# The first norm's second step and the scale of g called in the middle of the first group, and four more weight tiles ordered one behind the other, on one core

## The chip, the core and the metric

The kernel runs on one core of a Trainium2 chip. TensorE (PE in the profile) multiplies matrices, and loads their stationary side as PEld; VectorE (DVE), ScalarE (ACT) and GpSimd (POOL) work element by element; the queues of SyncE (SP), ScalarE and GpSimd issue the DMA transfers. The metric is the device time of one execution, in microseconds.

## The reference

Three layers follow one another, on 4 sequences of 576 tokens:

```python
attn = softmax(q @ k.T / 8 + cum[:, None] - cum[None, :], causal)   # 8 heads of 64; cum = cumsum(log f)
x  = heads joined to 512 columns of attn @ v
xn = (x - mean(x)) / sqrt(var(x) + 1e-6) * g_ln
x2 = x + relu(xn @ w_ch1) @ w_ch2                 # 512 x 2048 and 2048 x 512
u, v = split(relu(x2 @ w_in))                     # 512 x 1024
out = (u * (w_spatial @ layernorm(v) + b)) @ w_out
```

The weights of the MLPs arrive as 64-bit floats.

## The kernel before, in words

**Tiling.** The 2304 tokens are cut into nine blocks of 256 tokens (first, second and third part of a sequence, and a last block of leftovers). `BLOCKS` names their order. Attention of a block (`attention32` for the first two, `attention1` for the next two, `attention` for the rest) gives xT, 512 columns on partitions by 256 tokens. `GROUPS` makes eight groups of them, seven of one block and one of two; `mlp` runs the first MLP on a group. It has 16 steps j, one for each 128 of the 2048 hidden columns: the first layer into a bank ph (L858), relu into hh (L869, and hl at L873, what hh as a 16-bit number leaves over), the second layer into the banks acc (L843) two steps behind (`AHEAD`). Two banks hold ph, two hold acc. At a group's end the accumulators are scaled into t and added to x2 in memory (L890 or L892, and the DMA behind it).

**Precision.** The first group multiplies in fp32 with the weights as they are. All later groups multiply three times in fp16, with weights and inputs each as a high and a low part. xh and xl (L822) are the two parts of x, scaled by gs, one power of two times g.

**Weights.** The 16 weight tiles of 1 MB come as raw 64-bit words, three buffers deep. `load_w` converts tile j through `narrow`: ScalarE takes the upper word (L653) and the lower word (L654), VectorE clips (L655), fetches the sign (L656) and joins the two (L657). TensorE then sums the squares of a converted tile (L707, `squares`), and `scales` works out the two scales w1c and w2c from them when all tiles are there. `make16` halves a tile into its fp16 parts with them (ScalarE, and VectorE at L741).

**The first norm.** The first group doesn't wait for its norm: `norm`'s first step takes only the mean away from x times g, and keeps the mean in `kept`. The factor y, which is 1/sqrt(var + eps) for each token, is multiplied in at the end (L892). y comes out of the norm's second step: centre x (L776), square it (L782, ScalarE), two sums on GpSimd (L786, L787), a mean on TensorE, logarithm and exponential (L790, L791) and three corrections on VectorE (L792 to L794). The same lines serve the norm of every other block, where their c is xT with av in place of `kept`.

**The scale of g.** `gscale` loads g once more, 256 KB over all partitions, through GpSimd's queue (L249), takes the largest entry (L251), makes a power of two of it (L253, L261 to L263) and multiplies g by it (gs, L255). xh and xl need gs, and `scales` needs gsc.

**The order.** `run` gives every piece of work a number on a common axis, where the first group has 0 to 1, and calls the pieces sorted by it. A scheduler puts the instructions on each engine's queue in the order of the calls, its own estimate of when each can start, and the pairs that the code names with `after(later, earlier)`, which fixes an order and adds no work. The event that this case is about is

```python
events += [(at, -2, j) for j, at in enumerate(RAWAT)] + [(REST, -1, -1), (DEC, -1, -2)]
...
elif n < 0:
    drain(self.rest)
    self.gscale()
```

`self.rest` is the first norm's second step. The conversions of the tiles from 5 on stand at (j - 4.5)/17 on the axis, so 0.7 lies behind the one of the last tile, 15 (0.62); `scales` is at 0.76, the first halvings at 0.765. The names qk, s, sd, st, P, PT, vr, vp, vs, vq and vsc are attention's: scores s from qk (L530), a masked minimum (L535), P in two parts (L546), its transpose PT, and the product av<-PT,vp (L555), copied to xT (L556). vgram and vtr belong to a scale of v.

Of the kernel before, what the change touches and what calls it, by code (L numbers as in the profile page):

```python
# [57 lines left out]
PACE = (1, "x3", "split", "split", "split")  # L58
LOWAT = (1, "x3", "split")
SUMS = 14  # L60
REST = 0.7
SQ = (1, 3, 4, 5, 6, 8, 9, 10, 12, 13, 14, 16)
SOON = 5
WSC, MAKE, VN = 0.76, 0.765, 0.82
# [24 lines left out]
class Kernel:  # L89
# [586 lines left out]
    def load_w(self, j):  # L676

        nc = self.nc
        if j not in self.raw:
            self.load_raw(j)  # L680
        raw, w = self.raw.pop(j), self.wt[:, j + 2]
        low = self.st.tile([P, 2 * DM], U32, tag="low", name="low", bufs=2)
        joined = self.joined if 0 < j < 4 else None
        for hf in range(1 if j else 2):
            c = slice(0, 2 * DM) if j else slice(hf * DM, hf * DM + DM)
            first = self.narrow(raw[:, c], w[:, c], low[:, c], self.marks["split"] if hf else joined if j else self.marks["PT2"])
            if j == hf == 0:
                self.decays32(self.joined)
            for ins, pace in ((first, PACE), (self.low, LOWAT)):
                at = "x3" if hf else pace[j] if j < len(pace) else NP + j - len(pace) if ins is first else None  # L690
                if at is not None:
                    self.after(ins, self.marks[at] if isinstance(at, str) else self.done[at])
        self.marks[f"low{j}"] = self.low
        if j == 1:
            self.marks["w1"] = self.joined
        if j == 2:
            self.marks["third"] = self.joined
# [497 lines left out]
    def run(self):  # L1195
# [91 lines left out]
        events += [(WSC, -1, NF + 1)] + [(VN + 0.04 * i, -1, NF) for i in range(B + 2)]  # L1287
        events += [(at, -2, j) for j, at in enumerate(RAWAT)] + [(REST, -1, -1), (DEC, -1, -2)]
        events += [(BEGIN[-2] + M2A + (e + 0.5) / M2S, 2, last) for e in range(26)]
# [154 lines left out]
```

## Time and profile before

| | us |
|---|---|
| median of 3 runs | 788.42 (787.94 to 788.70) |
| the profiled execution | 784.56 |
| its span in the profile | 782.6 |
| TensorE busy | 754.1 |
| VectorE busy | 558.3 |
| ScalarE busy | 524.1 |

The first line is what is measured without a profile. The profiled execution is a single one; its span is from its first to its last instruction, and 2.0 us of its own time lie outside. The mean granted clock of TensorE over it was 0.991 of full speed. The first group runs to about 110 us, the second from there to 189 us.

### The profile page before, as it was taken

How to read it: one execution, taken by the hardware profiler on the slowest of the kernel's cores; microseconds unless marked ns; L12 is line 12 of the kernel's file. 1: busy time of each engine (PE TensorE's matmuls, PEld its weight loads, DVE VectorE, ACT ScalarE, POOL GpSimd, SP SyncE). 2: the span in 40 equal slices, each digit the busy share in tenths (PEclk: the TensorE clock that was granted, in tenths of full speed). 3: DMA queues.
4: the chain of work that ended last, by engine and by line, in shares of the span. 5: the costliest groups of instructions: out<-in, count | busy, mean ns of one | idle time of the engine just before them, and what ended most of it. 6: DMA issues, size and time to landing. Idle time of an engine off the chain costs nothing.

```text
span 782.6 us, 16305 instructions
## 1 busy us (share of the span) xinstructions
PE 754.1 (96%) x5966; PEld 578.2 (74%) x5966; DVE 558.3 (71%) x1508; ACT 524.1 (67%) x1320; POOL 67.7 (9%) x102
## 2 busy tenths in 40 slices
PE   8899996999999999899999999999999999999998
PEld 6699884887878787788878888544447678668676
DVE  7999899376699889969869846687515672654624
ACT  6998697475588978859759844475417743756543
POOL 5000111012201010110101100200021000000000
PEclk9999997899999999999999999999999999999999
DMA  9978953485779997967995755730043310100101
GB/s 260 309 266 271 285 156 60 72 192 87 220 149 185 197 206 174 206 151 157 184 198 113 126 80 182 194 130 29 1 79 73 106 62 1 39 23 17 47 1 61
DMA packets 164099, 104.69 MB, mean 134 GB/s; under 512 B 106146, under 2 KB 151298, under 8 KB 164020
## 3 DMA queue, kind: packets, MB, share of 16 engines
q1 hardware_dynamic: 157784, 96.60, 50.6%
q0 software_dynamic: 5376, 5.54, 5.4%
q10 hardware_dynamic: 860, 1.52, 0.6%
q8 instruction: 47, 0.77, 0.4%
q14 instruction: 32, 0.26, 0.1%
HBM read 64.37 MB, written 15.11 MB: 102 GB/s over the span
## 4 chain that ended last, share of the span: by engine, by line
PE 52%; DVE 15%; ACT 13%; issue 13%; DMA 6%; POOL 1%; SPq 0%; ACTq 0%; DVEq 0%; POOLq 0%
PE ph L858 11%; PE acc L843 11%; PE pb L803 7%; PE pb L804 7%; PE pb L802 7%; PE s L359 3%; PE av L582 3%; ACT wt L738 2%; DMA raw<-in_moe_w_ch_dram 1%; DVE x2z L342 1%; DVE sd L363 1%; ACT P L319 1%; ACT x L319 1%; DVE P L380 1%; ACT sd L367 1%
## 5 line engine op out<-in xcount | busy, mean ns | idle before, releaser
L843 PE MATMUL acc<-hh,wt 128*128 128x256 f16 (+2 forms) x960 | 198.3, 297 | 4.7 <-ACT hh L869 4.5
L858 PE MATMUL ph<-xh,wt 128*128 128x256 f16 (+1 forms) x896 | 186.8, 290 | 4.9 <-DVE hl L873 2.8
L843 PEld LDWEIGHTS <-wt 128*128 128x128 f16 x1344 | 130.2, 99 | 47.0 <-issue 8.3
L858 PEld LDWEIGHTS <-wt 128*128 128x128 f16 x1344 | 127.9, 99 | 49.3 <-issue 10.2
L858 PE MATMUL ph<-xl,wt 128*128 128x256 f16 (+1 forms) x448 | 129.7, 290 | 0.0
L843 PE MATMUL acc<-hl,wt 128*128 128x256 f16 (+1 forms) x416 | 116.2, 283 | 0.5 <-DVE hl L873 0.5
L869 ACT ACTIVATE hh<-ph 128x256 f16<-128x256 f32 (+2 forms) x128 | 50.8, 398 | 55.5 <-PE ph L858 54.8
L873 DVE SCALAR_TENSOR_TENSOR hl<-ph,hh 128x256 f16<-128x256 f32 (+1 forms) x112 | 50.8, 456 | 43.0 <-ACT hh L869 42.6
L319 ACT ACTIVATE P<-sd,st 128x512 f16<-128x512 f32 (+2 forms) x128 | 70.7, 587 | 8.0 <-DVE st L370 4.3
L367 ACT ACTIVATE sd<-sd,st 128x384 f32<-128x384 f32 (+2 forms) x80 | 54.6, 683 | 15.1 <-DVE st L363 14.8
L380 DVE SCALAR_TENSOR_TENSOR P<-sd,st,P 128x384 f16<-128x384 f32 (+2 forms) x96 | 58.4, 624 | 8.0 <-ACT P L319 7.3
L894 POOL DMA_DIRECT2D x_d<-t x36 | 32.6, 1080 | 219.4 <-DVE t L890 180.1
L359 PE MATMUL s<-x2z 128*128 128x384 f32 (+3 forms) x128 | 47.7, 381 | 2.1 <-DMA x2z<-decay_d 1.5
L363 DVE CUSTOM_DVE_ANT_0 sd<-s,mask 128x384 f32<-128x384 f32 (+2 forms) x80 | 46.0, 581 | 3.1 <-PE s L359 1.8
L359 PE MATMUL s<-x 128*128 128x384 f32 (+3 forms) x128 | 41.2, 331 | 0.0
L1170 DVE SCALAR_TENSOR_TENSOR u<-pb,wsc,u 128x288 f32<-128x288 f32 x32 | 16.1, 515 | 34.5 <-PE pb L1169 34.5
L802 PE MATMUL pb<-x2h,wil 128*128 128x288 f16 (+2 forms) x144 | 37.8, 273 | 0.0
L804 PE MATMUL pb<-x2h,wih 128*128 128x288 f16 (+2 forms) x144 | 37.7, 273 | 0.0
L803 PE MATMUL pb<-x2l,wih 128*128 128x288 f16 (+2 forms) x144 | 37.7, 273 | 0.0
L802 PE MATMUL pb<-wsh,vl 128*128 128x288 f16 x128 | 36.6, 286 | 0.3 <-ACT u L1110 0.2
L804 PE MATMUL pb<-wsh,vh 128*128 128x288 f16 x128 | 36.6, 286 | 0.0
L803 PE MATMUL pb<-wsl,vh 128*128 128x288 f16 x128 | 36.6, 286 | 0.0
(303 smaller groups left out, 1659.5 us busy)
## 6 DMA issues: line engine op xcount, KB each, us to landing
raw<-in_moe_w_ch_dram SPq DMA_DIRECT2D x32, 512.0 KB
qk<-in_qk_dram SPq DMA_DIRECT2D x32, 448.0 KB
vraw<-in_v_dram SPq DMA_DIRECT2D x5, 1024.0 KB
vr<-in_v_dram SPq DMA_DIRECT2D x16, 320.0 KB
x_d<-xT SPq DMA_DIRECT2D x9, 512.0 KB
x_d<-t POOLq DMA_DIRECT2D x36, 128.0 KB, 4.7
out_dram<-o SPq DMA_DIRECT2D x32, 144.0 KB
raw<-in_moe_w_in_dram SPq DMA_DIRECT2D x8, 512.0 KB
```

The source lines that it names most:

```text
L319: self.nc.scalar.activation(out, in_, AF.Copy, scale=scale)
L359: nc.tensor.matmul(ps[: R * u + R, : c1 - c0], lhsT=x[:, lo - q0 - R * u : hi - q0], rhs=y[:, c0:c1], start=g == 0, stop=g == len(heads[u] ...
L363: nc.vector.tensor_tensor_reduce(out=sd[:M, c0:c1], in0=ps[:M, : c1 - c0], in1=mask, scale=-0.125, scalar=3e38 if n == 0 else st[:M, n - 1 ...
L367: nc.scalar.activation(sd[:M, :N], sd[:M, :N], AF.Exp, bias=st[:M, n : n + 1], scale=-1.0, accum_out=st[:M, 2:3])
L380: low = nc.vector.scalar_tensor_tensor(out=dl, in0=src, scalar=rs, in1=dh, op0=ALU.mult, op1=ALU.subtract)
L802: first = mm(out, lhsT=al, rhs=bh, start=start, stop=False, **kw)
L803: mm(out, lhsT=ah, rhs=bl, start=False, stop=False, **kw)
L804: mm(out, lhsT=ah, rhs=bh, start=False, stop=stop, **kw)
L843: ins = nc.tensor.matmul(acc[m], lhsT=a, rhs=b, start=bank not in clear, stop=last and e == len(terms) - 1, skip_group_check=True)
L858: ins = nc.tensor.matmul(ph, lhsT=a, rhs=b, start=k == e == 0, stop=k == NK - 1 and e == len(terms) - 1)
L869: relu = nc.scalar.activation(hh, ph, AF.Relu)
L873: nc.vector.scalar_tensor_tensor(out=hl, in0=ph, scalar=0.0, in1=hh, op0=ALU.max, op1=ALU.subtract)
```

## The change

Two numbers change. `REST`, the place of the event above, goes from 0.7 to 0.35: the second step of the first norm and the whole of `gscale` are called between the conversions of tiles 10 and 11, ahead of the second block's last pieces. In `load_w`, the clip and the sign of tiles 4 to 7 are put behind the join of the tile before, as those of tiles 1 to 3 were already.

```diff
--- before.py
+++ after.py
@@ -58,7 +58,7 @@
 PACE = (1, "x3", "split", "split", "split")
 LOWAT = (1, "x3", "split")
 SUMS = 14
-REST = 0.7
+REST = 0.35
 SQ = (1, 3, 4, 5, 6, 8, 9, 10, 12, 13, 14, 16)
 SOON = 5
 WSC, MAKE, VN = 0.76, 0.765, 0.82
@@ -680,7 +680,7 @@
             self.load_raw(j)
         raw, w = self.raw.pop(j), self.wt[:, j + 2]
         low = self.st.tile([P, 2 * DM], U32, tag="low", name="low", bufs=2)
-        joined = self.joined if 0 < j < 4 else None
+        joined = self.joined if 0 < j < 8 else None
         for hf in range(1 if j else 2):
             c = slice(0, 2 * DM) if j else slice(hf * DM, hf * DM + DM)
             first = self.narrow(raw[:, c], w[:, c], low[:, c], self.marks["split"] if hf else joined if j else self.marks["PT2"])
```

In these orders a row is one instruction (or several alike, x2) with its line, operation and tiles. On VectorE, in the middle of the conversion, the difference has this piece (- before, + after; rows without a sign stand in both; e and st are attention's, gsc is the scale of g):

```order
-L655 TENSOR_SCALAR wt<-wt 128x1024
-L657 SCALAR_TENSOR_TENSOR wt<-wt,low 128x1024
-L656 SCALAR_TENSOR_TENSOR low<-raw,low 128x1024
+L262 TENSOR_SCALAR gsc<-gsc 128x1
+L657 SCALAR_TENSOR_TENSOR wt<-wt,low 128x1024
+L655 TENSOR_SCALAR wt<-wt 128x1024
+L656 SCALAR_TENSOR_TENSOR low<-raw,low 128x1024
+L263 TENSOR_SCALAR gsc<-gsc 128x1
+L776 TENSOR_TENSOR xT<-xT,kept 128x256 x4
+L255 TENSOR_SCALAR gs<-gT,gsc 128x4
```

The clip of a tile (L655) goes behind a join (L657), and the centring of the first norm (L776 with kept) and the steps of `gscale` stand here now, where before there were only conversions. On GpSimd's queue the load of g (L249) goes ahead of a memset and of two stores of the decays, behind the copies of the first values; the two sums (L786, L787) go ahead of the second of these stores.

On VectorE, at the seam of the first and the second group, ten rows of before around the end of y and the emptying of the banks (L892):

```order
L535 ISA sd,st<-s_1295,mask 128x256
L535 ISA st 128x1
L535 ISA sd,st<-s_1295,mask 128x256
L535 ISA st 128x1
L546 SCALAR_TENSOR_TENSOR P_1242<-sd,st,P_1242 128x2x128 x2
L794 SCALAR_TENSOR_TENSOR y<-t_1106,y 128x256
L539 RECIPROCAL st<-st 128x2
L892 TENSOR_TENSOR t<-y,acc 128x256 x2
L626 TENSOR_TENSOR ls<-xT 128x256
L892 TENSOR_TENSOR t<-y,acc 128x256 x2
```

and the rows of after around L892, directly behind the xl of the second group:

```order
L741 SCALAR_TENSOR_TENSOR wt<-wt,w1c 128x512
L741 SCALAR_TENSOR_TENSOR wt<-wt,w2c 128x512
L261 TENSOR_SCALAR vs<-s_1116 128x1
L741 SCALAR_TENSOR_TENSOR wt<-wt,w1c 128x512
L262 TENSOR_SCALAR vs<-vs 128x1
L741 SCALAR_TENSOR_TENSOR wt<-wt,w2c 128x512
L535 ISA sd,st<-s_1123,mask 128x256
L535 ISA st 128x1
L535 ISA sd,st<-s_1123,mask 128x256
L535 ISA st 128x1
L263 TENSOR_SCALAR vs<-vs 128x1
L892 TENSOR_TENSOR t<-y,acc 128x256 x2
```

L892 stands four halvings (L741) behind xl now, and no longer behind y's last correction (L794) and the third P of that stretch.

On TensorE, in the second group, before: acc_1532 is one of the banks that L892 empties, hh_1555 and hl_1556 are the hidden values of its first j, s2_1366 and s2_1391 are attention's, and the row above them (not shown) is the last product of av_1152.

```order
L274 MATMUL s2_1366<-vq_1363,ones_62 128x1
L530 MATMUL s2_1391<-qk_1359 128x256 x2
L843 LDWEIGHTS wt_171
L843 MATMUL acc_1532<-hh_1555,wt_171 128x256
L843 LDWEIGHTS wt_171
L843 MATMUL acc_1532<-hl_1556,wt_171 128x256
```

After, ph_1595 is the first layer of that group's second j, ph_1629 that of its third:

```order
L858 LDWEIGHTS wt_171
L858 MATMUL ph_1595<-xl_1531,wt_171 128x256
L858 LDWEIGHTS wt_171
L858 MATMUL ph_1595<-xh_1530,wt_171 128x256
L843 LDWEIGHTS wt_171
L843 MATMUL acc_1532<-hh_1555,wt_171 128x256
L843 LDWEIGHTS wt_171
L843 MATMUL acc_1533<-hh_1555,wt_171 128x256
L530 MATMUL s2_1295<-qk_1265 128x256 x2
L858 LDWEIGHTS wt_171
L858 MATMUL ph_1629<-xh_1524,wt_171 128x256
```

The second-layer products of the first j, which stood behind the three attention pieces av_1152, s2_1366 and s2_1391, now stand directly behind the first layer of the second j.

On TensorE, in the third group, the last products of the fourth block's attention (av_2299), before: ph_2780 is the first layer of the group's fifth j.

```order
L555 MATMUL av_2299<-PT_2264,vp_2245 64x128
L555 LDWEIGHTS vp_2245
L555 MATMUL av_2299<-PT_2264,vp_2245 64x128
L555 LDWEIGHTS vp_2245
L555 MATMUL av_2299<-PT_2264,vp_2245 64x128
L858 LDWEIGHTS wt_171
L858 MATMUL ph_2780<-xh_2550,wt_171 128x256
```

After, hh_2793 is the hidden value of that fifth j, so its second layer, which follows the first layer of the seventh:

```order
L555 MATMUL av_2299<-PT_2264,vp_2245 64x128
L555 LDWEIGHTS vp_2245
L555 MATMUL av_2299<-PT_2264,vp_2245 64x128
L843 LDWEIGHTS wt_171
L843 MATMUL acc_2558<-hh_2793,wt_171 128x256
L843 LDWEIGHTS wt_171
```

The same attention products stand behind the first layer of the seventh j, not of the fourth.

## Rows read from the trace of the kernel before

**Rows 1.** The page, part 1: busy us (share of the span) x instructions.
```profile
PE 754.1 (96%) x5966; PEld 578.2 (74%) x5966; DVE 558.3 (71%) x1508; ACT 524.1 (67%) x1320; POOL 67.7 (9%) x102
```

**Rows 2.** Windows: length; busy by engine (instructions); PE clock granted; DMA share; GB/s.
```profile
112.00:124.30 12.30, 9.23 (x86) 7.60 (x84) 12.30 (x37) 12.30 (x35) 0.82 (x1) 1.00 0.16 46
124.30:128.80 4.50, 4.45 (x24) 3.11 (x23) 4.50 (x13) 4.42 (x10) 0.00 (x0) 0.62 0.10 29
128.80:132.50 3.70, 0.00 (x0) 0.00 (x0) 3.70 (x12) 0.98 (x4) 0.00 (x0) 0.85 0.37 71
132.50:141.50 9.00, 8.08 (x49) 5.67 (x50) 5.58 (x21) 5.08 (x18) 3.62 (x4) 0.50 0.89 118
```

**Rows 3.** Timeline, PE: start, length (us), line, operands; idle before, releaser.
```profile
107.69 2.11 PE L843 MATMUL acc<-hh,wt 128*128 128x256 f32 x9
...
112.30 0.27 PE L858 MATMUL ph<-xh,wt 128*128 128x256 f16 x1
...
132.56 0.85 PE L555 MATMUL av<-PT,vp 128*64 128x128 f16 x12 [3.79 <-DVE P L546]
...
136.57 0.42 PE L843 MATMUL acc<-hh,wt 128*128 128x256 f16 x1
```

**Rows 4.** Timeline, DVE, second step of the first norm and around it.
```profile
105.29 1.42 DVE L776 TENSOR_TENSOR xT<-xT,kept 128x256 f32<-128x256 f32 x4
106.63 1.27 DVE L822 SCALAR_TENSOR_TENSOR xl<-xT,gs,xh 128x256 f16<-128x256 f32 x3
...
126.10 0.42 DVE L873 SCALAR_TENSOR_TENSOR hl<-ph,hh 128x256 f16<-128x256 f32 x1
...
132.48 0.42 DVE L794 SCALAR_TENSOR_TENSOR y<-t,y 128x256 f32<-128x256 f32 x1
...
132.97 0.73 DVE L892 TENSOR_TENSOR t<-y,acc 128x256 f32<-128x256 f32 x2
...
134.19 0.75 DVE L892 TENSOR_TENSOR t<-y,acc 128x256 f32<-128x256 f32 x2
```

**Rows 5.** Chain of waits, a piece at full clock: start, length, engine, tile, line.
```profile
151.16 1.31 PE ph L858 x12
```

**Rows 6.** Timelines of GpSimd and VectorE: load of g, squares' sums, weight halvings.
```profile
75.61 0.55 POOL L249 DMA_DIRECT2D gall<-in_moe_g_ln_dram  x1 [11.25 <-ACT wt L653]
...
110.06 1.62 POOL L786 TENSOR_TENSOR sq<-sq 128x512 f32<-128x512 f32 x1 [21.44 <-ACT sq L782]
...
109.14 0.74 DVE L741 SCALAR_TENSOR_TENSOR wt<-wt,w1c 128x512 f16<-128x512 f32 x1
109.81 0.74 DVE L741 SCALAR_TENSOR_TENSOR wt<-wt,w2c 128x512 f16<-128x512 f32 x1
110.63 1.61 DVE L741 SCALAR_TENSOR_TENSOR wt<-wt,w1c 128x512 f16<-128x512 f32 x1
112.16 1.22 DVE L741 SCALAR_TENSOR_TENSOR wt<-wt,w2c 128x512 f16<-128x512 f32 x1
```

**Rows 7.** A window early in the conversion, and ScalarE's timeline there.
```profile
16.00:18.00 2.00, 2.00 (x20) 1.98 (x20) 1.03 (x2) 0.83 (x2) 0.00 (x0) 1.00 1.10 380
...
31.77 1.16 ACT L653 ACTIVATE wt<-raw 128x1024 f32<-128x1024 f32 x1 [1.11 <-DMA raw<-in_moe_w_ch_dram]
```

**Rows 8.** Timelines of VectorE and PE: the last join, and its squares.
```profile
81.27 1.22 DVE L657 SCALAR_TENSOR_TENSOR wt<-wt,low 128x1024 uint32<-128x1024 uint32 x1
...
84.30 0.62 PE L707 MATMUL gram<-wt 128*128 128x128 bf16 x8
```

**Rows 9.** Timelines in the third to fifth group, and a window of 25 us.
```profile
199.25 0.37 ACT L556 ACTIVATE xT<-av,vsc 128x128 f32<-128x128 f32 x1 [1.39 <-PE av L555]
...
301.82 1.67 DVE L822 SCALAR_TENSOR_TENSOR xl<-xT,gs,xh 128x256 f16<-128x256 f32 x4
...
310.95 0.27 PE L858 MATMUL ph<-xh,wt 128*128 128x256 f16 x1
...
300.00:325.00 25.00, 22.21 (x211) 17.74 (x209) 23.51 (x66) 22.31 (x58) 3.97 (x6) 1.00 0.94 170
```

## The prediction

> **What bounds the kernel now.** The page first: TensorE is busy for 754.1 of 782.6 us [rows 1], so the end moves by what TensorE loses: idle time, and work at its lower clock. The windows show that nearly half of that loss stands in one place, between the first group and the second [rows 2]. From 112 to 141.5 us TensorE is idle for 3.07, 0.05, 3.70 and 0.92 us (length less busy time, window by window), 7.7 us in all. It also runs at 1.2 GHz for much of this: with a granted clock c, work of the length t would have taken c x t at full clock, so 4.45 x 0.38 = 1.7 and 8.08 x 0.50 = 4.0 us are lost, 5.7 together. **13.4 us** are lost there. The idle time came first, and the clock was lower behind it.
>
> Then who was late. On TensorE [rows 3] the first group's last second-layer product ends about 109.8 us, the second group's first product runs at 112.30, but that group's first second-layer product (L843 with f16) only at 136.57. It needs the accumulator banks, and L892 empties these; L892 ran at 132.97 and 134.19 [rows 4], directly behind L794, which writes y at 132.48. y is the last value of the first norm's second step, and that step began only at 105.29 (L776). The banks were full for 23 us with nothing to do but wait for y. Beside it, TensorE stood 3.79 us before L555 at 132.56, and that row names the P of L546 for it [rows 3]: VectorE was late with everything, being busy for all of 112 to 132.5 us [rows 2].
>
> **The change part by part.**
>
> *y earlier.* The xl of the second group (L822) end at 107.90 today, with L776 among them [rows 4]; without its 1.42 us they end at 106.5. In the new order four weight halvings (L741) and two masks follow, then two L892, one more L741, and the other two L892. L741 follows upon L741 after 0.66 us [rows 6]; a mask takes half of that, as an estimate. So the two pairs of L892 run near 109.8 and 111.3, where the last product ends (109.8). The second-layer products of the second group then stand between its first-layer ones, and TensorE has work in every stretch where it now has none. Does VectorE follow? Out of its full stretch go L776 (1.42), L792 to L794 (three like L794's 0.42) and the collision below (1.35), 4.0 us; in come the four L892 (1.5, now at 133). So the third hl, at 126.10 today, comes some 2.5 us earlier, about 123.6, and the fourth one behind an L281, two L741, two masks and a P, by these rows some 3.4 us later: 127.4. TensorE needs that fourth hl for the sixth j, whose first product goes into the bank (two hold ph) that this hl frees. It takes 12 products in 1.31 us [rows 5], and is there at 112.3 + 2.5 (attention pieces and a mean that now stand ahead, an estimate) + 5 x 1.31 + 3 x 1.31 + 3 (other pieces, an estimate) = 128.3. VectorE is just in time; a wait of 0 to 1 us is left. I take the whole **13.4** as gained and put the doubt into the next terms.
>
> *The load of g earlier.* L249 now stands behind the copies of v on GpSimd's queue, near 12.6 us, with nothing to wait for; today it issues at 75.61 [rows 6]. The DMA engines are full in the first 36 us (share 1.10 at 16 us), and ScalarE waits 1.11 us at 31.77 for weights [rows 7]. 256 KB at the 380 GB/s of that time are 0.7 us. Bounds 0 (other loads wait anyway) and 1.0 (at 260 GB/s); I take **+0.7**. The maximum (L251) and the four small steps cost what they did, elsewhere.
>
> *The step itself in the middle of the conversion.* L776 (1.42 on VectorE), L782 (1.05 on ScalarE) and the two sums on GpSimd (L786, L787) now run near 51 to 60 us, among the conversions of tiles 7 to 9. There is a collision: at 110.06 the two sums lay over L741, which took 1.61 and 1.22 us for its usual 0.74 [rows 6], 1.35 us more; L656 and L657 have two inputs in SBUF as L741 has. The Trainium skill (SBUF — State Buffer, Who interferes with whom) says that VectorE with two SBUF inputs and a GpSimd instruction that reads SBUF take one port in turn, the loser blocked for the whole instruction; by it one blocked instruction could wait out the whole first sum, 1.62 us, in place of the 1.35 of both, and the sum below would be 0.3 us worse. The trace agrees with the direction; the price I use is the row's. So the last converted tile is late by up to 1.42 + 1.35 = 2.8 us. Cover: today it is ready at 82.5 (81.27 + 1.22) and its square product starts at 84.30 [rows 8], 1.8 us. What is over reaches TensorE: **+1.0**, bounds 0 (the waits of ScalarE, and of VectorE behind it, for weights still on their way take it up) and 2.8. L782 on ScalarE goes into the same waits.
>
> *The tiles one behind the other.* Tiles 4 to 7 clip behind the join of the tile before. Same instructions; VectorE has other work in the swapped places, and the join now stands before a clip that would wait for ScalarE's L653 anyway. **0**, at most the one clip's length either way, which I put at L741's 0.7 us [rows 6] for as many elements.
>
> *What comes back later.* The order shows the price: attention's pieces fall behind the products. The last L555 of the fourth block stands behind the fourth j of the third group today, and behind the seventh afterwards: 3 j of 2 x 1.31 are 7.9 us. So when the products are about 12 us earlier (13.4 - 1.7), that block's end, 199.62 today [rows 9], is only about 4 earlier, and the fifth block, whose loads wait for it, too. Its xl is finished at 303.5 and first read at 310.95 [rows 9], 7.5 us spare: 12 - 4 - 7.5 is about nothing. But from 300 to 325 us VectorE is already busy for 23.5 of 25 us and TensorE idle for 2.8 [rows 9], and attention has to catch up there. Bounds 0 and 7.9; I take **+2.5**, nearer to the low end because TensorE had the spare time to its own queue and the orders meet again by the fifth group.
>
> Sum: -13.4 + 0.7 + 1.0 + 0 + 2.5 = **-9.2 us**. Against the profiled execution's own 784.56 that is 775.4; this execution lies 3.9 us under the median of the runs, 788.42, and I carry the difference over: **779.2 us**.
>
> **Rivals.** (A) Attention keeps the lag: block five is the pace up to the sixth group, the whole 7.9 us come back, with up to 2.1 more in the two conversion terms. Gain 1.8 to 5.5, 783 to 786.6. For it: VectorE and the DMA engines are about full in 300 to 325 us; against it, 400 to 500 us is TensorE's alone, and the bound 7.9 assumes no catching up. (B) y was not the last: TensorE stood for P at 132.56. If P stays late behind the halvings, the 3.70 us idle and the 4.0 behind it at 1.2 GHz stay: gain about 13.4 - 7.7 less half the other terms, 4, so 784. Against it: in the new order the P of that piece stands before the third hl, and the second-layer products are ahead of L555. (C) Slower: attention does not move at all. If the fifth block starts at today's time, the products have to wait out their 12 us at the fourth to sixth groups' starts in stretches of 3 to 5 us, and each such stop is followed by half speed, as here (3.70 idle, then 4.0 lost). Three stops cost up to 8 us that are paid nowhere today: 788.4 + 1.7 + 3 or so, 791 to 796. It decides when attention's shift is under what the clock takes, some 2 us; the order's 4 speaks against it. (D) Nothing: the terms cancel, 788.
>
> **Numbers.** Forecast (gain over 5.5 us) 0.66, A 0.13, B 0.08, C 0.08, D 0.05. Range: low end with nothing given back, 788.42 - 13.4 = 775; high end with every bound paid, -13.4 + 1.0 + 2.8 + 7.9 = -1.7, 786.7, which takes in A and B and leaves out about 0.13 above and a few hundredths below. The likeliest case by itself is 775 to 783. 0.2% is 1.6 us, about what a measurement here can tell from no change: faster 0.87, same 0.05, slower 0.08.
>
> **What would show it.** Right: in the new profile L892 runs by 113 us and L843 with f16 before 122; TensorE's idle time between 110 and 145 us is under 2 us and the granted clock stays at 1.00; L251 does not wait for its load; the last L657 is at 81 to 84; the fourth block's last L556 is 3 to 6 us earlier than today, the group after it by 8 to 12. Wrong: a granted clock near 0.5 anywhere behind 110 us, new waits of TensorE for L656 or L657 before 85 us, or xl (L822) of the fifth to seventh groups arriving with TensorE waiting for it.

## The result, and the profile after

The changed kernel takes 778.57 us in the median of 4 runs (773.79 to 778.85), the kernel before beside it 788.18 (784.40 to 788.70): a ratio of 0.9874, with a 95% interval of 0.9825 to 0.9923. On a second chip (experiment e6 below) it was 778.08 against 786.14, a ratio of 0.9907 (0.9883 to 0.9931). The forecast was 779.2 us. The total came out as forecast, in part by luck: its terms did not, and most of this text is about that.

Page of the changed kernel, the span and part 1 [rows 1]:

```profile
span 777.0 us, 16306 instructions
PE 749.2 (96%) x5966; PEld 575.1 (74%) x5966; DVE 555.1 (71%) x1508; ACT 524.5 (68%) x1320; POOL 67.2 (9%) x102
```

TensorE's idle time (span less busy) is 27.8 us, where it was 28.5: nearly the same. It is busy for 4.9 us less with the same 5966 products. So in this pair of profiles the gain of 5.6 us is almost all a higher clock. The windows of the seam, with the bounds of [rows 2]:

```profile
112.00:124.30 12.30, 10.78 (x109) 9.16 (x109) 12.17 (x37) 12.30 (x33) 3.59 (x4) 1.00 0.76 154
124.30:128.80 4.50, 4.50 (x43) 4.06 (x42) 4.50 (x11) 4.50 (x11) 0.00 (x0) 1.00 0.13 37
128.80:132.50 3.70, 2.52 (x24) 2.10 (x23) 3.70 (x11) 3.63 (x8) 0.00 (x0) 1.00 0.37 71
132.50:141.50 9.00, 8.74 (x91) 7.17 (x89) 8.16 (x27) 6.59 (x24) 0.00 (x0) 1.00 0.16 31
```

The clock is 1.00 throughout; TensorE is idle for 1.52, 0.00, 1.18 and 0.26 us, 3.0 in all. VectorE is still busy nearly all the time. TensorE's timeline there [rows 3]:

```profile
113.69 1.46 PE L843 MATMUL acc<-hh,wt 128*128 128x256 f32 x6
...
116.75 0.53 PE L555 MATMUL av<-PT,vp 128*64 128x128 f16 x12 [0.79 <-DMA PT<-P]
...
118.48 0.27 PE L858 MATMUL ph<-xh,wt 128*128 128x256 f16 x1
...
122.15 0.38 PE L843 MATMUL acc<-hh,wt 128*128 128x256 f16 x2
...
124.13 0.27 PE L858 MATMUL ph<-xh,wt 128*128 128x256 f16 x1 [0.73 <-DVE hl L873]
...
130.92 0.27 PE L858 MATMUL ph<-xh,wt 128*128 128x256 f16 x1 [1.18 <-DVE hl L873]
```

The second group's second layer starts 3.7 us behind its first layer (122.15 against 118.48), where 24.3 us lay between them. But the group itself starts 6.2 us later than before (118.48 against 112.30), since the first group ends later (115.2 against 109.8). Its own end, by the first L890, is 6.0 us earlier (182.6 against 188.6). VectorE's timeline [rows 4, 8]:

```profile
52.16 1.42 DVE L776 TENSOR_TENSOR xT<-xT,kept 128x256 f32<-128x256 f32 x4
...
57.43 1.69 DVE L655 TENSOR_SCALAR wt<-wt 128x1024 f32<-128x1024 f32 x1
59.15 1.17 DVE L237 SCALAR_TENSOR_TENSOR dec<-cum,dec 32x576 fp32r<-32x576 f32 x1
...
81.33 0.69 DVE L655 TENSOR_SCALAR wt<-wt 128x1024 f32<-128x1024 f32 x1 [2.04 <-ACT wt L653]
...
84.55 1.22 DVE L657 SCALAR_TENSOR_TENSOR wt<-wt,low 128x1024 uint32<-128x1024 uint32 x1
...
89.07 0.42 DVE L792 SCALAR_TENSOR_TENSOR t<-av,y 128x256 f32<-128x256 f32 x1 [3.30 <-ACT y L791]
...
116.50 0.74 DVE L892 TENSOR_TENSOR t<-y,acc 128x256 f32<-128x256 f32 x2
...
117.82 0.74 DVE L892 TENSOR_TENSOR t<-y,acc 128x256 f32<-128x256 f32 x2
...
130.46 0.41 DVE L873 SCALAR_TENSOR_TENSOR hl<-ph,hh 128x256 f16<-128x256 f32 x1
...
134.07 0.41 DVE L873 SCALAR_TENSOR_TENSOR hl<-ph,hh 128x256 f16<-128x256 f32 x1
```

L892 runs directly behind the first group's end, as the order promised; the last two rows are the third and the fourth hl of the second group. The last join ends at 85.8, 3.3 us later than before. And there is a wait that the prediction did not have. y's first correction comes only at 89.07, because on ScalarE the exponential L791 stands behind an L272 that waits for attention's values:

```profile
83.74 0.48 ACT L790 ACTIVATE y<-av,eps 128x256 f32<-128x256 f32 x1 [0.42 <-PE av L751]
...
88.22 0.42 ACT L272 ACTIVATE vp<-vr 128x256 f16<-128x256 f32 x1 [4.01 <-DMA vr<-in_v_dram]
...
88.64 0.40 ACT L791 ACTIVATE y<-y 128x256 f32<-128x256 f32 x1
```

The step holds the bank av from its mean until L792 reads it. TensorE's next product into av, the mean of the second block, waits for that:

```profile
36.75 1.99 PE L843 MATMUL acc<-hh,wt 128*128 128x256 f32 x8 [1.11 <-ACT hh L869]
...
89.55 0.70 PE L751 MATMUL av<-ls,onesf 128*128 128x256 f32 x2 [1.57 <-DVE t L792]
```

The first row is the mark of the early load of g: ScalarE stood 2.28 us for weights before its L653 at 32.72, 1.11 before [rows 7].

### The profile page after: what moved, and what is told of

It is laid out like the page before. It is cut to its first block, busy times and chain, and to the rows that moved or that the text cites. A ratio compares the mean times of both kernels' runs of the same rounds, so it can differ in the third digit from the quotient of the medians.

```text
span 777.0 us, 16306 instructions
## 1 busy us (share of the span) xinstructions
PE 749.2 (96%) x5966; PEld 575.1 (74%) x5966; DVE 555.1 (71%) x1508; ACT 524.5 (68%) x1320; POOL 67.2 (9%) x102
## 3 DMA queue, kind: packets, MB, share of 16 engines
q10 hardware_dynamic: 860, 1.52, 0.6%
## 4 chain that ended last, share of the span: by engine, by line
PE 60%; DVE 16%; ACT 10%; DMA 9%; issue 4%; SPq 1%; DVEq 0%; ACTq 0%
PE ph L858 14%; PE acc L843 12%; PE pb L803 8%; PE pb L804 8%; PE pb L802 8%; PE s L359 3%; DMA raw<-in_moe_w_ch_dram 3%; PE av L582 2%; DMA vr<-in_v_dram 2%; PE s L843 1%; DVE wt L741 1%; DMA raw<-in_moe_w_in_dram 1%; DMA qk<-decay 1%; ACT P L319 1%; DVE low L656 1%
## 5 line engine op out<-in xcount | busy, mean ns | idle before, releaser
L843 PE MATMUL acc<-hh,wt 128*128 128x256 f16 (+2 forms) x960 | 196.6, 295 | 3.3 <-ACT hh L869 3.2
L858 PEld LDWEIGHTS <-wt 128*128 128x128 f16 x1344 | 126.9, 98 | 49.7 <-issue 12.4
L843 PEld LDWEIGHTS <-wt 128*128 128x128 f16 x1344 | 128.5, 98 | 43.8 <-issue 5.8
L843 PE MATMUL acc<-hl,wt 128*128 128x256 f16 (+1 forms) x416 | 115.3, 281 | 1.2 <-DVE hl L873 1.2
L319 ACT ACTIVATE P<-sd,st 128x512 f16<-128x512 f32 (+1 forms) x128 | 70.1, 587 | 8.8 <-DVE st L370 5.6
L380 DVE SCALAR_TENSOR_TENSOR P<-sd,st,P 128x384 f16<-128x384 f32 (+1 forms) x96 | 58.5, 630 | 11.1 <-ACT P L319 10.2
L802 PE MATMUL pb<-wsh,vl 128*128 128x288 f16 x128 | 36.6, 286 | 0.1
L804 PE MATMUL pb<-wsh,vh 128*128 128x288 f16 x128 | 36.6, 286 | 0.0
L803 PE MATMUL pb<-wsl,vh 128*128 128x288 f16 x128 | 36.6, 286 | 0.0
```

What stands on the lines that cost most here:

```text
L319: self.nc.scalar.activation(out, in_, AF.Copy, scale=scale)
L380: low = nc.vector.scalar_tensor_tensor(out=dl, in0=src, scalar=rs, in1=dh, op0=ALU.mult, op1=ALU.subtract)
L802: first = mm(out, lhsT=al, rhs=bh, start=start, stop=False, **kw)
L803: mm(out, lhsT=ah, rhs=bl, start=False, stop=False, **kw)
L804: mm(out, lhsT=ah, rhs=bh, start=False, stop=stop, **kw)
L843: ins = nc.tensor.matmul(acc[m], lhsT=a, rhs=b, start=bank not in clear, stop=last and e == len(terms) - 1, skip_group_check=True)
```

## The experiments

Executions of one kernel on one chip differ by 4 to 7 us, those of e9 by 10, so the comparisons go by the ratio of all runs of one job, with its interval. The table has them all; times in us. Idle is TensorE's window length less its busy time, clock is the granted clock from 110 to 145 us, and the three windows, the first L892 and the end of the last join (L657) come from the profiled execution of each.

| kernel | median | ratio to before (95%) | span of the profile | first L892 | last join | idle 0-110 | idle 110-145 | clock | idle 145-400 |
|---|---|---|---|---|---|---|---|---|---|
| before | 788.18 | | 782.6 | 133.0 | 82.5 | 6.29 | 7.74 | 0.80 | 8.66 |
| e1 before, again | 784.73 (one run) | | 782.8 | 132.8 | 82.2 | 6.56 | 7.83 | 0.80 | 7.66 |
| after | 778.57 | 0.9874 (0.9825-0.9923) | 777.0 | 116.5 | 85.8 | 9.46 | 2.96 | 1.00 | 9.22 |
| e6 after, again | 778.08 | 0.9907 (0.9883-0.9931) | 773.4 | 116.2 | 85.5 | 8.31 | 2.97 | 1.00 | 8.80 |
| e2 step early, g late, tiles | 777.96 | 0.9884 (0.9861-0.9907) | 776.4 | 112.6 | 83.9 | 7.10 | 3.70 | 1.00 | 7.72 |
| e3 g early, step late, tiles | 783.77 | 0.9973 (0.9959-0.9987) | 781.4 | 135.2 | 83.7 | 7.52 | 6.76 | 0.80 | 7.93 |
| e4 tiles alone | 781.45 | 0.9942 (0.9921-0.9962) | 781.8 | 136.8 | 83.9 | 6.32 | 8.13 | 0.80 | 7.28 |
| e7 tiles alone, again | 781.75 | 0.9948 (0.9929-0.9967) | 780.7 | 136.3 | 84.0 | 6.47 | 4.99 | 0.71 | 7.52 |
| e5 step and g early, tiles free | 776.15 | 0.9870 (0.9847-0.9892) | 776.6 | 114.9 | 86.4 | 7.18 | 2.33 | 0.95 | 7.85 |
| e10 step early, g late, tiles free | 774.59 | 0.9872 (0.9844-0.9899) | 773.2 | 111.5 | 84.2 | 6.93 | 3.01 | 1.00 | 7.84 |
| e8 after, y ahead | 778.83 | 0.9906 (0.9884-0.9928) | 777.5 | 111.0 | 86.7 | 7.31 | 1.31 | 0.95 | 10.13 |
| e12 y ahead, tiles free | 778.00 | 0.9907 (0.9880-0.9934) | 775.6 | 110.5 | 86.8 | 7.31 | 1.42 | 1.00 | 10.51 |
| e11 both at 0.5, tiles free | 782.29 | 0.9956 (0.9935-0.9977) | 780.8 | 112.0 | 85.8 | 6.89 | 1.57 | 0.95 | 12.43 |
| e9 before, hole filled | 786.97 | 1.0031 (1.0007-1.0055) | 785.0 | 134.3 | 82.4 | 6.00 | 7.50 | 0.90 | 9.81 |

The kernel before ran beside them at 786.17 (e1 to e4), 786.14 (e5 to e8) and 785.32 us (e9 to e12).

**e1, the kernel before once more.**

> The kernel before, unchanged, for a second profile: its first profiled execution (784.56 us) lay 3.9 us under the median of its runs. My theory of the change: the loss at the seam of the first two groups is the same in every execution (7.7 us idle and 5.7 at 1.2 GHz between 112 and 141.5 us, shifted by where the group starts), so a slower execution (about 788.4) differs elsewhere, by some 4 us in the stretch where weights are loaded (before 85 us). Rival: the seam itself varies, and the slower execution has 4 us more there, so that part of the measured gain is this variation.

The seam is the same to 0.1 us in both profiles, and so are the ends of the groups (188.6 and 188.8 for the second, 494.6 and 494.9 for the seventh). Both profiled executions are below most runs of the kernel; where the others spend their time could not be seen here, since e1's trace is of a short one as well. So neither the expectation on the slower executions nor the rival, a seam that varies, was tested: all that is shown is that two short executions have the same seam.

**e2, the step early and the scale of g late.** The event is split in two:

```diff
-REST = 0.35
+REST, RESTG = 0.35, 0.7
-events += [...] + [(REST, -1, -1), (DEC, -1, -2)]
+events += [...] + [(REST, -1, -1), (RESTG, -1, -3), (DEC, -1, -2)]
...
-                    drain(self.rest)
-                    self.gscale()
+                    rest = drain if n == -1 else lambda g: self.gscale()
+                    rest(self.rest)
```

> The first norm's second step at 0.35, the scale of g left at 0.7, the weight tiles as in the changed kernel. My theory: the whole gain comes from y being ready when the first group ends, so 778 us here too, perhaps 0.7 less because g is loaded late again (776.5 to 780.5), with L892 right behind the second group's xl and no stop of TensorE over 2 us at the seam. Rival (it is the earlier scale of g, which xh and xl need, that lets the second group start): 787 to 789.

777.96: the gain is there without the early g. The wait near 37 us is gone (idle 0 to 110 is 7.10, not 9.46), and so is the one before L751.

**e3, the scale of g early and the step late.** The same edit with `REST, RESTG = 0.7, 0.35`.

> The reverse: the scale of g at 0.35, the first norm's second step left at 0.7, the weight tiles as in the changed kernel. My theory: the banks wait for y as before, so TensorE loses 11 to 14 us at the seam again, and the early load of g adds some 0.7: 787.5 to 790.5. Rival (the scale of g is what counts): 778 to 782.

The seam is as before, as my theory has it (window with the columns of [rows 2]):

```profile
110.00:145.00 35.00, 28.24 (x226) 21.40 (x225) 30.98 (x88) 28.01 (x77) 6.21 (x6) 0.80 0.44 79
```

L892 waits for y until 135.2, TensorE is idle for 6.8 us and has a clock of 0.80. With y late the seam is bad, whatever g does. The time, 783.77, is nevertheless 2.4 us under the kernel before and outside what I expected. The tiles, which it has too, explain that (next run); against the tiles alone, the early g costs 2.3 us (783.77 less 781.45), with intervals that just touch.

**e4 and e7, the order of the tiles alone.**

```diff
-        joined = self.joined if 0 < j < 4 else None
+        joined = self.joined if 0 < j < 8 else None
```

> Only the order of the weight tiles 4 to 7 (one behind the other), both steps at 0.7 as before. My theory: no effect beyond 0.7 us, 787.5 to 789.5, the seam as before. Rival (the tiles in order let the last one be converted sooner, and a good part of the gain is theirs): under 786, with the last join (L657) over 1 us earlier than in the kernel before.

> Only the order of tiles 4 to 7, once more, for a second profile and a second interval. If the 4.7 us of the first time are its own: 0.992 to 0.996 of the kernel before again, and a profile shorter than that of before by more than the 1 us of the first. If they were chance of the executions: 0.997 to 1.001.

Faster by 4.7 and 4.4 us on two chips: the rival's time, but not its reason. The last join is 1.4 to 1.5 us later, not earlier, and the seam is no better:

```profile
110.00:145.00 35.00, 26.87 (x197) 20.81 (x197) 31.53 (x93) 28.15 (x76) 5.96 (x6) 0.80 0.47 93
```

That is e4's. Idle time and lost clock are 8.13 + 0.20 x 26.87 = 13.5 us here, 4.99 + 0.29 x 30.01 = 13.7 in e7, and 7.74 + 0.20 x 27.26 = 13.2 before. What differs is later: the third group ends 5.1 and 2.9 us later than before (252.2 and 250.0 against 247.0), but xl of the fifth and sixth groups begins 2.4 to 5.4 us earlier (299.4 and 356.0, 296.6 and 353.6, against 301.8 and 359.0), and the seventh group ends at 494.6 and 492.9 against 494.6. So the order has moved attention ahead of products. The two profiles are only 0.8 to 2.1 us shorter than those of before, so that they don't show where the rest of the 4.5 lies; that stays open.

**e5, the step and g without the tiles.** `REST = 0.35` alone, `0 < j < 4` as before.

> Only the moved step and scale of g (at 0.35), tiles 4 to 7 free as before. My theory as predicted, with the tiles worth nothing: as fast as the changed kernel, 9 to 10 us under the kernel before on this chip. Rival (additive, after the run with only the tiles, which was 4.7 us faster: the tiles give 4 to 5 of the 9.6): only 4 to 6 us under the kernel before. Second rival (the two gains overlap): 8 to 10 us here although the tiles alone give 4.

776.15: the whole gain without the tiles, the second rival. **e6** is the changed kernel beside it:

> The changed kernel, unchanged, on the same chip as its parts and with a second profile: ratio to the kernel before 0.986 to 0.990. The wait that the first profile showed should be there again: TensorE some 1.6 us before the mean L751 near 89.5 us for the bank av, which L792 frees late because the exponential L791 stands on ScalarE's queue behind an L272 that waits for its values; and some 1.1 us before L843 near 37 us, with the load of g early.

Both waits are there again (1.39 us before L751 at 89.23, 0.89 before L843 at 36.6). With the step moved, the tiles' order no longer gains: 0.9870 without and 0.9907 with it here, 0.9872 and 0.9884 with g late (e10 and e2), 0.9907 and 0.9906 with y ahead (e12 and e8). No pair shows a difference beyond its intervals, and none a gain.

**e10, the step alone.** e2's split with the tiles free.

> The first norm's second step at 0.35, the scale of g at 0.7, tiles 4 to 7 free as before: the moved step by itself. If the gain is y's alone, and the early load of g costs 1 to 2 us and the tiles nothing or less: as fast as the step and g together without the tiles, or up to 2 us faster; 0.984 to 0.988 of the kernel before. Rival (the tiles' order is needed as well): 0.990 to 0.994.

774.59, 0.9872: as fast as with g and step together. So of the change's three parts the step carries all of the gain that the runs can tell. Whether this version is faster than the changed kernel itself isn't shown: the two did not run side by side, and the intervals of their ratios overlap.

**e8, y ahead.** One more order:

```diff
-        nc.scalar.activation(y, y, AF.Exp, scale=-0.5)
+        self.marks.setdefault("y0", nc.scalar.activation(y, y, AF.Exp, scale=-0.5))
...
-            nc.scalar.activation(h, v, AF.Square, accum_out=ss)
+            self.after(nc.scalar.activation(h, v, AF.Square, accum_out=ss), self.marks["y0"])
```

> The changed kernel with one order added: the first L272 of the third block, which waits for its values, stands behind the exponential L791 of the first norm, not ahead of it. My theory (TensorE's 1.57 us before L751 at 89.5 come from that queue, and the first group ends later by them): that wait is gone, and the second group starts 1 to 2 us earlier; 0.5 to 2 us faster than the changed kernel on this chip. Rival (the time is paid later anyway, because the attention of the fifth block sets the pace of the fifth group): the second group starts earlier, but the end stays within 0.5 us.

The wait before L751 is gone, and the second group starts at 114.23 and not at 117.98 (e6). The time is the same, 778.83 against 778.08. The windows of e8 show where it went:

```profile
110.00:145.00 35.00, 33.69 (x314) 28.05 (x313) 31.71 (x95) 29.93 (x82) 3.56 (x4) 0.95 0.49 101
145.00:400.00 255.00, 244.87 (x2250) 202.29 (x2249) 200.69 (x557) 194.64 (x519) 27.48 (x39) 0.99 0.86 174
```

1.7 us less idle time at the seam than in e6, 1.3 more behind it (10.13 against 8.80), in stops of attention: 1.38 us for qk at 171.6, 2.07 for P at 249.4, 2.14 for PT at 392.0. The lower clock at the seam, 0.95, takes another 0.05 x 33.69 = 1.7 us, which e6 did not lose. The rival's result, if not just its place. **e12** is the same with the tiles free:

> Both steps at 0.35, tiles free as before, and the first L272 of the third block behind the exponential L791. If the tiles cost something beside the moved step (776.2 without them, 778.1 with them on the last chip), this is 1 to 2 us faster than with them (778.8): 0.985 to 0.989 of the kernel before. If that difference was chance: 0.990 to 0.992.

778.00, 0.9907: no faster than with the tiles, with 10.51 us idle from 145 to 400 us.

**e11, both steps at 0.5.** `REST = 0.5`, tiles free.

> Both steps at 0.5, tiles free as before. y is then still ready long before the first group ends, and the load of g stands behind the fullest stretch of the DMA engines. My theory: the seam as with 0.35, and the waits before 45 us as in the kernel before: 0.984 to 0.988. Rival (what counts is where the scheduler then puts the attention of later blocks, not these steps): anywhere between 0.985 and 0.995, with the same idle time at the seam.

The rival. y is ready at 95.4, long before the first group ends, L892 runs at 112.0, about as early as in e10, the seam has the least idle time but two, and still only 3 us of the gain are left. Windows of e11:

```profile
110.00:145.00 35.00, 33.43 (x315) 27.64 (x315) 30.49 (x92) 28.32 (x77) 3.62 (x4) 0.95 0.43 83
145.00:400.00 255.00, 242.57 (x2196) 199.32 (x2195) 203.23 (x563) 195.81 (x524) 27.66 (x39) 0.98 0.83 172
```

and of e10, which has the whole gain:

```profile
110.00:145.00 35.00, 31.99 (x313) 26.53 (x312) 31.80 (x95) 29.57 (x82) 3.60 (x4) 1.00 0.42 81
145.00:400.00 255.00, 247.16 (x2274) 203.01 (x2271) 206.43 (x569) 197.14 (x528) 28.82 (x39) 0.99 0.87 177
```

Idle time behind the seam is 12.43 against 7.84 us, and the clock is lower as well. Three stops make most of it. Their windows, and TensorE's row at the first of them:

```profile
160.00:180.00 20.00, 17.22 (x128) 13.53 (x127) 18.28 (x66) 17.78 (x63) 1.74 (x2) 0.91 0.67 135
265.00:280.00 15.00, 12.86 (x106) 9.60 (x104) 11.42 (x32) 11.90 (x30) 0.20 (x1) 0.89 0.91 200
385.00:395.00 10.00, 8.17 (x69) 6.18 (x68) 6.83 (x21) 5.66 (x17) 0.20 (x1) 0.83 1.04 191
```

```profile
173.88 1.13 PE L530 MATMUL s<-qk 66*128 66x256 f32 x4 [2.14 <-DMA qk<-in_qk_dram]
```

Idle there is 2.78 + 2.14 + 1.83 = 6.8 us, and the lower clock takes 0.09 x 17.22 + 0.11 x 12.86 + 0.17 x 8.17 = 4.4 more. In e10 the same three windows have 1.5 us idle and a clock of 1.00.

**e9, the hole filled.** In the kernel before, 32 products of ones go into the bank that the late L555 will overwrite:

```diff
-                pav = self.bank("av")[:, :P]
+                pav = self.bank("av")[:, :P]; [mm(pav, lhsT=self.ones.bitcast(BF16)[:, :P], rhs=self.ones.bitcast(BF16)[:, :P], start=True, stop=True) for _ in range(32 * (b == 0 and p == n == 1))]
```

> The kernel before, with 32 products of ones (128x128, bf16) put into the bank av ahead of the L555 that TensorE waits for at 132.5 us; the first real product overwrites them. They begin when L792 frees that bank (about 128.7) and last 3.4 us at 1.2 GHz, so they fill the 3.7 us hole with work that is worth nothing. My theory (of the 13.4 us, 4.0 are the lower clock that follows on this hole): idle time at the seam falls by 3 us or more, the granted clock from 132.5 to 141.5 is above 0.9 and not 0.50, L892 stays where it is, and the kernel is 2 to 4 us faster although it does more. Rival (the clock is not governed by that hole, or stays low whatever TensorE does there): the clock there stays near 0.50, and the time within 1 us of the kernel before.

It failed as a test. The windows of [rows 2], and three rows of TensorE:

```profile
112.00:124.30 12.30, 9.43 (x89) 7.82 (x88) 12.30 (x37) 12.30 (x35) 0.47 (x1) 1.00 0.16 44
124.30:128.80 4.50, 3.07 (x32) 2.50 (x30) 4.50 (x13) 4.06 (x9) 0.00 (x0) 1.00 0.10 29
128.80:132.50 3.70, 1.47 (x27) 1.41 (x25) 3.70 (x11) 1.09 (x4) 0.00 (x0) 1.00 0.52 75
132.50:141.50 9.00, 8.02 (x58) 6.02 (x58) 4.17 (x18) 3.73 (x14) 3.62 (x4) 0.62 0.72 99
```

```profile
123.96 0.27 PE L858 MATMUL ph<-xh,wt 128*128 128x256 f16 x1 [2.12 <-DVE vs L263]
...
128.33 1.95 PE L550 MATMUL av<-ones 128*128 128x128 bf16 x32 [0.64 <-DVE t L792]
...
132.63 0.85 PE L555 MATMUL av<-PT,vp 128*64 128x128 f16 x12 [2.35 <-DMA PT<-P]
```

The clock stayed at 1.00 behind the stop of 2.12 us this time, so the filler took 1.95 us and not 3.4, and a stop of 2.35 us remained. Behind it the clock fell again, to 0.62 instead of 0.50. That is no rule: in e3 a stop of 2.39 us before an L555 at 131.11 was followed by 0.53 from 132.5 to 141.5. The hole was never really filled, and the kernel was 1.7 us slower, with 1.2 us more idle time from 145 to 400 us (9.81) and 2.3 more from there to the end: the edit had put other work in another order too. It tells nothing against the clock term, and does not show it.

## Why the prediction was right, and where it was not

**y earlier, −13.4.** The mechanism was right: the banks waited for y, and only the runs with an early step are rid of most of the loss (e2, e5, e10 against e3, e4, e7). Idle time and lost clock at the seam, reckoned as above, are 12.4 to 13.7 us in every run with the step late (before, e1, e3, e4, e7; e9, with its filler, left aside) and 1.4 to 4.0 in every run with it early. In e3 the first second-layer product waits for L892 itself, 0.54 us before 135.95. Moving the step also takes its own work out of VectorE's full stretch, and frees there the bank av, which it held from its mean at 118.19 to L792 at 128.22. No run does one of these without the others; that it was y is read from the traces.

The lower clock went entirely: 0.80 to 1.00 from 110 to 145 us, 0.20 x 27.26 = 5.5 us, against 5.7. Of the idle time only 7.74 − 2.96 = 4.8 us went, against 7.7. "A wait of 0 to 1 us is left" was too low: the third and fourth hl came at 130.46 and 134.07, not at 123.6 and 127.4, and TensorE waited 0.73, 1.18 and (at 134.5) 0.26 us for hl and 0.79 for PT. The sum is −10.3: this step was mis-sized by 3 us, because the group itself started 6 us later than before, and VectorE, for which 2.5 us less work had been reckoned, was as full as before (20.37 of the 20.5 us from 112 to 132.5, after 20.50).

**The load of g early, +0.7.** ScalarE stood 1.2 us longer for weights at 32 us, and TensorE 1.1 us behind it (0.9 in e6). In time, 2.3 us between e3 and e4, hardly beyond their intervals, and nothing that can be told between e5 and e10.

**The step in the conversion, +1.0.** The collision took 1.42 us, against 1.35: L655 took 1.69 for its 0.69 beside the first sum, and L237 behind it 1.17 beside the second, where it takes 0.75 in the kernel before. The last join ended 3.3 us later than before, at 85.8, where 81 to 84 was forecast; the table has parts of that: 1.4 with the tiles alone (e4), 1.7 with the step alone (e10), 3.9 with step and g (e5). Not seen at all was the price of this order: y's step is cut in two by ScalarE's queue, and holds the bank av for over 5 us (83.7 to 89.5). The place alone doesn't bring it: in e2 and e5 the step has the same place and an L272 ahead of L791 too, but that L272 waits 1.86 us in e2 and not at all in e5, and TensorE has no such stop. TensorE's idle time from 0 to 110 us rose by 3.2 us (2.0 in e6) where 1.7 were forecast for both terms.

**The tiles, 0.** Wrong by themselves (−4.5 us, twice), and right beside the moved step, where no gain is left of them. Why, is open. The bound, a clip's length put at L741's 0.7 us "for as many elements", was right by luck: a clip has 1024 columns, L741 512, and takes 0.69 us all the same.

**What comes back later, +2.5.** Attention did what I feared: the last L556 of the fourth block ended at 199.54, not 3 to 6 us earlier than today's 199.62, and xl of the fifth group was finished at 304.6, a microsecond later than before. It cost little, because the spare 7.5 us of the fifth group's xl took it up: TensorE is idle for 0.6 us from 300 to 325 us (24.41 busy of 25.00), where it was 2.8 [rows 9]. Idle time behind 145 us was 0.9 us more than before (0.5 less in e6), and a clock of 0.97 from 300 to 350 us took 0.03 x 47.6 = 1.4 (none in e6). So 2.3, and −0.5 in the second profile.

The sums are −10.3 + 3.2 + 2.3 = −4.8 for the first profile (span 5.6 us shorter) and −10.2 + 2.0 − 0.5 = −8.7 for the second (9.2 or 9.4 shorter). The medians, over more executions, have −9.6 and −8.1. The forecast of −9.2 thus had a gain that was 3 us too large, against price terms of 4.2 in sum, where the two profiles show 5.5 and 1.5, partly in other places. That the median came within 0.6 us of the forecast is therefore partly luck. Profile against profile it was not so close: 775.4 us were forecast for the profiled execution, and it took 778.85; the 3.9 us that were carried over to the median are not in it, and where they lie stays open.

Of the signs named beforehand, the clock at the seam (1.00) and L251, which waits for nothing, came out. L892 (116.5), the idle time (2.96), the last join (85.8) and the fourth block's end missed their marks, and L843 (122.15) missed its own by a hair. One sign of being wrong showed, further on: behind a stop of 1.78 us before an L582 at 330.88 the clock was 0.70 from 330 to 335 us. In e6 a stop of 1.94 us at the same place left it at 1.00.

**The rivals.** Attention's lag (A) is real, and e11, e8 and e12 show it as a danger: with a y as early, these orders give up to 8 us back in attention's stops. (B) did not happen: no L555 at the seam waited for more than 0.79 us. (C) took its premise, attention that doesn't move, from the right place, and e11's three stops with their lower clock (11 us together) are what it describes; the changed kernel has five stops of 1.0 to 1.8 us from 145 to 400 us, and only behind the one at 330.88 the clock fell.

## What to carry to other kernels

Look for the last value that a full bank waits for, and who is late with it: a chain of small steps that nothing on the path needs until then can be called far earlier. Here an earlier start was enough; whether a faster chain would have done as well (in the kernel before it took 27.6 us, from 105.29 to 132.90) was not tried. Count a stop of TensorE twice, as idle time and as the work that the rows show at half clock behind it; here the second was the larger gain (5.5 us against 4.8). It does not follow every time: in e9 the clock stayed at 1.00 behind 2.12 us. And where a scheduler sets the order, expect an edit of one place to move work in all later ones: a stop removed at one seam is kept only if the orders further on have no new one, which e11 against e10 shows at 8 us for the same seam.

## What the runs showed of the hardware that was not expected

The granted clock differs from one execution of a program to the next: in the 17 runs of the kernel before in the job of e1 to e4 it was from 0.988 to 0.995, and the span from 786.2 to 781.5 us along with it. The same stop of 2.12 us before the same instruction was followed by a clock of 0.62 and 0.63 in the two profiles of before [rows 2] and by 1.00 in e9.

VectorE's clip (L655), which has one tensor as input, was held up by GpSimd's sum as the two-input L741 had been [rows 6]: 1.69 us for 0.69. The Trainium skill (SBUF — State Buffer, SBUF: two separate sides) counts among the instructions that share the port with GpSimd also those in a mode that uses two ports, and says that the loser waits for the whole of the other. The trace agrees: L655 was issued at 57.43, L786 ran until 58.57, and L655 ended at 59.12, 0.55 us behind it. That L655 is in such a mode the trace doesn't say; it handles 1024 columns in 0.69 us where L741 takes 0.74 for 512. GpSimd's rows of the two sums:

```profile
56.82 1.75 POOL L786 TENSOR_TENSOR sq<-sq 128x512 f32<-128x512 f32 x1 [29.76 <-ACT sq L782]
58.65 1.06 POOL L787 TENSOR_TENSOR sq<-sq 128x256 f32<-128x256 f32 x1
```

The first of them began while L656, with its two inputs, was still running (56.21 to 57.43), and took 1.75 us, where the sum at 95.05 takes 1.26.
